# Attention scores in runs of one and a half key tiles over six PSUM banks

## The chip, the cores and the metric

The kernel runs on one core of one Trainium2 chip. The metric is the time of one execution on the device in microseconds (us), the median of several. TensorE (PE in the profile; PEld its weight loads), VectorE (DVE), ScalarE (ACT), GpSimd (POOL) and SyncE (SP, which issues most DMA transfers) each work through a queue of their own, in order, and wait for one another through semaphores. TensorE writes into PSUM, eight banks of 128 partitions by 512 float32 numbers, from which ScalarE and VectorE read.

## What is computed

Two layers, each of an attention block and a spectral filter, on 2048 rows of 1024 numbers:

```python
def _A_ref(x, wqkv, wo):                 # 32 heads of 32 numbers
    qkv = (x @ wqkv).reshape(B, S, 3, H, Dh) ...
    scores = einsum("bhqd,bhkd->bhqk", q, k) * (Dh ** -0.5)
    p = softmax(scores)
    o = einsum("bhqk,bhkd->bhqd", p, v)
    return o.transpose(...).reshape(B, S, D) @ wo
x = x + _A_ref(layernorm(x), wqkv, wo)
x = x + _B_ref(layernorm(x), w_r, w_i)   # rfft2, times a weight, irfft2
x = x + _A_ref(layernorm(x), wqkv, wo)
x = x + _B_ref(layernorm(x), w_r, w_i)
```

The change touches the attention block alone.

## The kernel before

**Tiles.** The 32 heads are worked on in eight groups of four (g = 0 to 7), the 2048 queries in four chunks of 512 (c), the 2048 keys in 16 tiles of 128 (kt). One *unit* is one (g, c, kt): 64 units a group. Float32 products are made of float16 parts, high and low, in three terms: high by high, high by low, low by high. The head's 32 numbers are the contraction, so the score matmuls use strips of 32 rows of the array, one strip for each head of the group.

**A unit.** `S` (line 697) makes the scores of a unit: three terms by four heads, each a matmul of 32 rows, 128 keys and 512 queries. They go into two tiles `s` of the pool `psS`, each of two banks and two heads; the pool has three such tiles, six banks in all. `S` also issues two exps on ScalarE (line 701), one for each tile, into tiles `p` of a pool of eight. `PV` (line 707) multiplies four heads' `p` by V, 128 rows by 32 columns, in float32, two passes each, into one bank `o`, accumulated over the 16 key tiles of the chunk. `add` (lines 718 and 720) sums `p` over the key tiles into `acc` on VectorE, two instructions of 128x1024 a unit. At a chunk's end `fin` (from line 727) sums `acc` over partitions with a matmul by ones, turns and inverts the sums on VectorE, and scales the output; `out` splits it into float16 parts (line 740 on ScalarE, 741 on VectorE) and stores it through SyncE's queue (line 743).

**What goes between.** Beside the units, TensorE makes q, k and v of later groups. `filler` yields step by step: a sum of q or k (`qk_chunk`, line 420) is 24 matmuls of 512 columns in 24 steps, a sum of v (`v_tiles`, line 465) 48 of 256 columns in 24 steps; both accumulate in the only tile `x` of the pool `psX`. At a sum's end the result is split: a high part by ScalarE (line 215), a low part by VectorE (line 216); for q and k the square of the high part is taken as well, for norms (line 427 on VectorE, line 425 on ScalarE where g is 7). Even groups make k, q and k (12 sums), odd groups 1, 3 and 5 make q and v (4 and 8 sums), group 6 makes k and q of group 7 and begins with the output projection (`wo_parts`, line 526). `prep` loads the weights of the next phase in pieces (line 301, SyncE) into three buffers and splits each (lines 215, 216). When the four sums of a phase are done, `norms` (line 440) adds the squares up by a matmul into a tile of `psS`, and VectorE takes the maximum (line 442), from which the exp's bias comes.

**Order.** TensorE's and ScalarE's instructions are issued in the order of the program; a planner orders the other queues by when it believes that things are ready. The order is: `S` of a unit; with every even unit the `PV` of the two units before it; with every odd unit a slot of filler, eight steps mostly and twelve at times (`slots` spreads the sums over the group). At the first unit of a chunk `fin` of the chunk before follows its last `PV`. In the trace, TensorE's order is therefore: S, PV PV, S, filler, S, PV PV, S, filler.

Of the kernel before, what the change touches and what calls it, by code (L numbers as in the profile page):

```python
# [104 lines left out]
SQ = 2.0 ** 5  # L105
# [131 lines left out]
class AttnPools:  # L237


    def __init__(self, tc):  # L240
        self.tc = tc
        self.low = Pools(tc, "left")
        self.big = self.low("at_x", 1).tile([128, 16384], F32, name="big")
        self.right = Pools(tc, "right")
        r = self.right("at_r", 1).tile([128, 16384], F32, name="R")
        self.x = r.rearrange("p (t d) -> p t d", d=1024)
        k = r.bitcast(F16).rearrange("p (t a n) -> p t a n", a=2, n=2048)
        self.k = [k[:, i] for i in (3, 4, 5)]
# [3 lines left out]
        a = r.rearrange("p (a j n) -> p a j n", j=2, n=512)  # L252
        self.acc = [a[:, i] for i in (14, 15)]

    def close(self):
        self.small.close()
# [19 lines left out]
class Weights:  # L276
# [6 lines left out]
    def prep(self, ph, mid=None):  # L283
        nc, ap, wp = self.nc, self.ap, self.wp
        kind, g = ph
        if kind == "v":
# [19 lines left out]
            load()  # L306
        yield
        for i, (h, l, _) in enumerate(sl):
            split(nc, h, l, st[i], SW)
            load()  # L310
            yield
        if self.flag is not None:
            v = w[:, 0].rearrange("p d n -> p (d n)")
# [17 lines left out]


SPILL = [2, 3, 8, 9]
PH0 = [("v", 0), ("k", 0), ("q", 0)]


def attention(nc, tc, layer, ap, xin, yd, wts, wo, cst, dram, flags):
# [69 lines left out]
    def qk_chunk(ph, c):  # L407
# [13 lines left out]
            if i < 23:  # L421
                yield
        split(nc, t[:, 0], t[:, 1], ps, SQ / (SX * SW))
        if g == NG - 1:
            nc.scalar.activation(nrm[ph][:, c], t[:, 0], AF.Square)
        else:
            (nc.gpsimd if both else nc.vector).tensor_tensor(nrm[ph][:, c], t[:, 0], t[:, 0], op=ALU.mult)
        if c == 3:
            left_norms.append(ph)
        yield  # L430

    left_norms = []

    def norms():
        kind, g = ph = left_norms.pop(0)
        if g not in mx:
            mx[g] = sm.tile([128, 2], F32, name="mqk")
        ps = psS.tile([128, 2, 512], F32, name="s")
        for c in range(4):
            nc.tensor.matmul(ps[32 * c:32 * c + 32, 0], cst["bones"], nrm[ph][:, c], start=True, stop=True)  # L440
        i = 0 if kind == "k" else 1
        nc.vector.reduce_max(mx[g][:, i:i + 1], ps[:, 0], axis=AX.X)  # L442
        if kind == "q":
            mkbias(g)

# [31 lines left out]
    def sums(ph):  # L477
        return 8 if ph[0] == "v" else 4

    def filler():  # L480
        for i, ph in enumerate(phases[:-2]):
            nxt = (s for p in phases[i + 1:i + 2 + (i + 4 > len(phases))] for s in prep(p))
            for n in range(sums(ph)):
# [202 lines left out]
    both.clear()  # L686


    P, O, acc = {}, {}, ap.acc

    def S(g, c, kt):

        s = [psS.tile([128, 2, 512], F32, name="s") for _ in range(2)]
        for i, (a, b) in enumerate(((0, 0), (0, 1), (1, 0))):
            for h in range(4):
                r = slice(32 * h, 32 * h + 32)
                nc.tensor.matmul(s[h // 2][:, h % 2], K[g][r, a, kt * 128:kt * 128 + 128],  # L697
                                 Q[g][r, b, c * 512:c * 512 + 512], start=i == 0, stop=i == 2)
        for hf in range(2):
            p = P[g, c, kt, hf] = pp.tile([128, 2, 512], F32, name="p")  # L700
            nc.scalar.activation(p, s[hf], AF.Exp, bias=bias[g], scale=SCALE / (SQ * SQ))  # L701

    def PV(g, c, kt):
        if kt == 0:
            O[g, c] = psO.tile([128, 512], F32, name="o")
        for h in range(4):
            nc.tensor.matmul(O[g, c][32 * h:32 * h + 32], V[g][:, kt, 32 * h:32 * h + 32], P[g, c, kt, h // 2][:, h % 2],  # L707
                             start=kt == 0, stop=kt == NKT - 1)
# [5 lines left out]
    def add(g, c, kt):  # L714
        for hf in range(2):
            p = P[g, c, kt, hf]
            if kt == 1:
                nc.vector.scalar_tensor_tensor(acc[hf], P[g, c, 0, hf], 1e-34, p, op0=ALU.add, op1=ALU.add)  # L718
            elif kt:
                last_add = nc.vector.tensor_add(acc[hf], acc[hf], p)  # L720
        return last_add if kt > 1 else None

    def fin(g, c):
        zt = on.tile([128, 16, 32], F32, name="zt")
        z = psS.tile([128, 2, 512], F32, name="s")[:, 0]
        for h in range(4):
            nc.tensor.matmul(z[32 * h:32 * h + 32], cst["ones"], acc[h // 2][:, h % 2], start=True, stop=True)  # L727
        nc.vector.transpose(zt.rearrange("p a b -> p (a b)"), z)  # L728
        rc = sm.tile([128, 16], F32, name="rc")
        nc.vector.reciprocal(rc, zt[:, :, 0])  # L730
# [3 lines left out]
        nc.vector.scalar_tensor_tensor(r, O[g, c], SO, r, op0=ALU.mult, op1=ALU.mult)  # L734
        O[g, c] = r

    def out(g, c, eng=nc.vector):
# [3 lines left out]
        eng.tensor_tensor(t[:, 1], r, t[:, 0], op=ALU.subtract)  # L741
        if g < NG - 1:
# [4 lines left out]
    pend, done, late = [], [], []  # L747
    fill, lwo, wof = filler(), load_wo(), wo_parts()
    left, rests = 16, {}
# [4 lines left out]
    def slots(f, sums, n, steps):  # L754

        while sums:
            k = max(1, int(n / sums + 0.5))
            m = -(-steps // k)
            for i in range(0, steps, m):
                while left_norms:  # L760
                    norms()
                for _ in range(min(m, steps - i)):
                    next(f, None)
                n -= 1
                yield sums - (i + m >= steps)
            sums -= 1

    with tc.manual_schedule(engines={mybir.EngineType.PE, mybir.EngineType.Activation}):
        for g in range(NG):
            todo = sum(sums(ph) for ph in beside.get(g, []))  # L770
            sl = slots(fill, todo, 22 if g == NG - 2 else 32, 24)
            wsl = slots(wof, 4, 10, 21)
            for u in range(NCH * NKT):
                c, kt = divmod(u, NKT)
                S(g, c, kt)
                if g == u == 0:
                    run(last_v)
                if kt % 2 == 0:
                    for w in pend:
                        PV(*w)  # L780
                    late = pend
                    pend = []
                    if kt == 0 and late:
                        for w in late:
                            last_add = add(*w)
                        with tc.issue_after(last_add.ins):
                            wts.look()
                        done = [late[1][:2]]
                        fin(*done[0])
                        late = []  # L790
                for w in late[:1]:
                    add(*w)
                late = late[1:]
                if kt == 5 and done:
                    out(*done.pop())
                pend.append((g, c, kt))
                if kt % 2 == 0:
                    continue
                if todo:
                    todo = next(sl)  # L800
                elif g == NG - 2:
                    if left:
                        run(lwo)
                        left = 0
                    if next(wsl, None) is not None and u == NCH * NKT - 1:
                        run(wsl)
                elif g == NG - 1:
                    for _ in range(share[u // 2]):
                        next(wof)
                    if u // 2 in rests:  # L810
                        wo_rest(rests[u // 2])
                if g == NG - 2 and todo <= 6 and left > (8 if todo > 4 else 0):
                    next(lwo)
                    left -= 1
        for w in pend:
            PV(*w)
        for w in late + pend:
# [3 lines left out]
    with tc.manual_schedule(engines={mybir.EngineType.PE}):  # L821
# [40 lines left out]
            for _ in range(n):  # L862
                next(folds, None)
        first(0, range(7))
        fin(NG - 1, NCH - 1)
        out(NG - 1, NCH - 1, nc.vector)
        some(6)
        first(1, range(7))
# [512 lines left out]
```

## Time and profile before

| | |
|---|---|
| median of 3 runs | 3764.36 us (3763.21 to 3766.41) |
| the profiled execution | 3764.43 us, its span 3762.6 us |
| TensorE busy | 3695.4 us, 98% of the span |
| VectorE busy | 3218.8 us, 86% |
| ScalarE busy | 2900.2 us, 77% |
| GpSimd busy | 298.8 us, 8% |
| granted TensorE clock, mean | 0.996 |
| 2048 exps (line 701) | 2170.0 us busy, 1112 ns each |
| 1792 additions (line 720) | 2088.6 us busy, 1220 ns each |
| head groups 1 to 6 of the first layer | 178.0 to 180.2 us each |

Busy times of one engine are added up over the span; durations of neighbouring instructions on an engine overlap a little, so what one costs is the distance from its start to the next start. TensorE's ends are modelled: a matmul of 512 columns is shown 0.38 us long, while the next starts 0.22 us after it. In a timeline row, the first number is the start, the second the length of the merged instructions, then engine, line, operation, output and inputs, and how many were merged; in brackets stands idle time of the engine and who ended it.

### The profile page before, as it was taken

Reading aid. Unit: us, or ns where it says so; the run is one execution under the profiler, and the core shown is the slowest. Engines: PE = TensorE matmul, PEld = TensorE weight load, DVE = VectorE, ACT = ScalarE, POOL = GpSimd, SP = SyncE. Lnnn points to the kernel's source line nnn. Section 1 sums busy time; section 2 is a strip of 40 time slices with the busy share of each in tenths; the row PEclk is TensorE's granted clock in tenths of the full one; section 3 lists DMA queues with packets and bytes.
Section 4 is the critical chain, followed back from the end, with each engine's and each line's share of the span. In section 5 each row is a group of like instructions: output and inputs, shape, how many; then the busy total and the mean of one; then the engine's idle time right before and its main releaser. Section 6 shows DMA issues by size and latency. Waiting matters only on the chain.

```text
span 3762.6 us, 80259 instructions
## 1 busy us (share of the span) xinstructions
PE 3695.4 (98%) x33271; PEld 1637.1 (44%) x33271; DVE 3218.8 (86%) x3874; ACT 2900.2 (77%) x3587; POOL 298.8 (8%) x388
## 2 busy tenths in 40 slices
PE   8999999999999999999999999999999999999998
PEld 5333433343343333378963334333433433333788
DVE  7899899989999988975658998999899999789755
ACT  5788888888888866658748888888888888666686
POOL 1000000000000000014410000000000000000243
PEclk9999999999999999999999999999999999999999
DMA  6000000000000211233250000101000102111423
GB/s 194 10 18 18 13 13 17 26 7 18 13 27 15 88 54 65 74 143 106 70 157 21 29 29 24 32 24 35 14 29 29 41 15 85 54 71 68 166 86 109
DMA packets 150119, 198.43 MB, mean 53 GB/s; under 512 B 58224, under 2 KB 104048, under 8 KB 148720
## 3 DMA queue, kind: packets, MB, share of 16 engines
q1 hardware_dynamic: 148416, 192.62, 15.8%
q8 instruction: 263, 4.31, 0.5%
q14 instruction: 112, 0.92, 0.1%
q10 hardware_dynamic: 1328, 0.59, 0.1%
HBM read 132.35 MB, written 48.23 MB: 48 GB/s over the span
## 4 chain that ended last, share of the span: by engine, by line


## 5 line engine op out<-in xcount | busy, mean ns | idle before, releaser
L701 ACT ACTIVATE p<-s,bias 128x1024 f32<-128x1024 f32 x2048 | 2170.0, 1112 | 563.0 <-PE s L697 545.6
L720 DVE TENSOR_TENSOR R<-R,p 128x1024 f32<-128x1024 f32 x1792 | 2088.6, 1220 | 131.2 <-ACT p L701 126.8
L707 PE MATMUL o<-p,R 128*32 128x512 f32 x8192 | 985.0, 598 | 0.0
L420 PE MATMUL x<-big,wqk 128*128 128x512 f16 x2880 | 676.5, 380 | 2.3 <-ACT R L469 1.9
L697 PEld LDWEIGHTS <-R 32*128 32x128 f16 x12288 | 230.9, 92 | 749.2 <-issue 633.5
L420 PEld LDWEIGHTS <-wqk 128*128 128x128 f16 x3072 | 275.6, 98 | 418.4 <-issue 129.3
L707 PEld LDWEIGHTS o<-p,R 128*32 128x32 f32 x8192 | 213.6, 109 | 523.4 <-issue 523.4
L697 PE MATMUL s<-Q,R 32*128 32x512 f16 x6144 | 427.3, 377 | 4.6 <-DVE R L567 2.7
L697 PE MATMUL s<-R 32*128 32x512 f16 x6144 | 430.4, 377 | 1.5 <-ACT p L701 0.3
L465 PE MATMUL x<-wv,big 128*128 128x256 f16 x2784 | 330.6, 275 | 4.1 <-DVE R L216 2.2
L465 PEld LDWEIGHTS <-big 128*128 128x128 f16 x3072 | 290.9, 98 | 100.2 <-issue 59.3
L526 PE MATMUL x<-big 128*128 128x512 f16 x1050 | 241.6, 380 | 0.0
L448 POOL PARTITION_ALL_REDUCE mall<-mqk x16 | 38.4, 2401 | 2278.1 <-DVE mqk L442 2266.7
L526 PEld LDWEIGHTS <-big 128*128 128x128 f16 x1344 | 124.3, 98 | 176.4 <-issue 38.6
L718 DVE SCALAR_TENSOR_TENSOR R<-p 128x1024 f32<-128x1024 f32 x128 | 150.8, 1218 | 31.8 <-ACT p L701 31.8
L1043 DVE TENSOR_TENSOR H<-G,H 128x512 f16<-128x512 f32 (+1 forms) x68 | 47.0, 692 | 119.8 <-ACT H L1042 119.6
L988 ACT COPY U<-ps 64x256 f32<-64x256 f32 (+1 forms) x272 | 97.2, 357 | 9.2 <-PE ps L995 3.9
L988 ACT COPY B<-ps 64x256 f32<-64x256 f32 (+1 forms) x272 | 97.2, 357 | 5.4 <-PE ps L995 1.7
L995 PE MATMUL ps<-cbi,H 128*128 128x256 f16 (+1 forms) x792 | 98.6, 273 | 1.5 <-DVE H L1043 1.0
L728 DVE STREAM_TRANSPOSE zt<-s 128x512 f32<-128x512 f32 x64 | 45.8, 715 | 62.6 <-PE s L727 62.5
L995 PE MATMUL ps<-cb,big 128*128 128x256 f16 x780 | 96.7, 273 | 0.0
L995 PEld LDWEIGHTS <-H 128*128 128x128 f16 (+1 forms) x792 | 76.5, 98 | 12.4 <-DVE H L1043 2.4
(443 smaller groups left out, 2981.7 us busy)
## 6 DMA issues: line engine op xcount, KB each, us to landing
wst<-in_wp SPq DMA_DIRECT2D x96, 256.0 KB, 3.0
R<-y SPq DMA_DIRECT2D x32, 512.0 KB, 5.2
w<-in_w SPq DMA_DIRECT2D x60, 256.0 KB, 2.7
od<-ohl SPq DMA_DIRECT2D x56, 256.0 KB, 2.4
big<-od SPq DMA_DIRECT2D x16, 896.0 KB, 5.9
y<-R SPq DMA_DIRECT2D x20, 512.0 KB, 2.6
wst<-in_wo SPq DMA_DIRECT2D x32, 256.0 KB, 2.7
xres<-in_x SPq DMA_DIRECT2D x16, 512.0 KB, 3.6
```

The costliest lines, as they stand in the source:

```text
L420: nc.tensor.matmul(ps, a, b, start=i == 0, stop=i == 23)
L465: nc.tensor.matmul(ps[:, j], x[c][:, d, o:o + 128], w[:, n, d], start=i == 0, stop=i == 23)
L526: nc.tensor.matmul(p, a, b, start=start and d == ds[0] and i == 0, stop=stop and d == ds[-1] and i == 2)
L697: nc.tensor.matmul(s[h // 2][:, h % 2], K[g][r, a, kt * 128:kt * 128 + 128], Q[g][r, b, c * 512:c * 512 + 512], start=i == 0, stop=i == 2)
L701: nc.scalar.activation(p, s[hf], AF.Exp, bias=bias[g], scale=SCALE / (SQ * SQ))
L707: nc.tensor.matmul(O[g, c][32 * h:32 * h + 32], V[g][:, kt, 32 * h:32 * h + 32], P[g, c, kt, h // 2][:, h % 2], start=kt == 0, stop=kt == ...
L718: nc.vector.scalar_tensor_tensor(acc[hf], P[g, c, 0, hf], 1e-34, p, op0=ALU.add, op1=ALU.add)
L720: last_add = nc.vector.tensor_add(acc[hf], acc[hf], p)
L728: nc.vector.transpose(zt.rearrange("p a b -> p (a b)"), z)
L988: nc.scalar.copy(ov[64 * r:64 * r + 64, a0:a0 + m, x], tl[64 * x:64 * x + 64, :m, r])
L995: nc.tensor.matmul(out, l, r, start=k == 0, stop=k == len(mm_) - 1)
L1043: nc.vector.tensor_sub(lo, gs, hi)
```

## The change

In groups 0 to 6, the 16 units of a chunk are made in ten runs `S3` and one plain `S`. An S3 makes the scores of one whole unit and of one half (256 queries) of another: of each three key tiles, the first and the third are whole units, the middle one is made in two halves. It takes all three tiles of `psS`: `y` (heads 2, 3 of the whole unit), `z` (four heads of the half unit, two heads in each bank) and `x` (heads 0, 1 of the whole unit), and three exps follow in the order y, z, x. The order of its 24 matmuls is written out in `RUN`: heads 0 and 1 begin with their half, heads 2 and 3 with their whole. The two pairs use the banks of `z` one after the other; a wait goes over SyncE's queue, a `nop` that waits for heads 0 and 1 and for which heads 2 and 3 wait.

Three `PV` units follow every second run, fillers of twelve steps follow the other runs and the first. The last unit of a chunk is left over and multiplied in the first run of the next, with `fin` behind it. Half units have `PV` of 256 columns and an addition `add_half` of both pairs of heads at once. The norms' matmuls move in between the `PV` units and write into the bank of the fillers; squares are made on ScalarE for all q and k within these groups. SyncE's queue joins the ones in program order, the output is stored two runs after its split, and `prep` loads a weight piece ahead of the next split instead of behind the last. Group 7 keeps the old order.

```diff
-        self.acc = [a[:, i] for i in (14, 15)]
+        self.acc = r.rearrange("p (a j n) -> p a j n", j=2, n=512)[:, 14:16]
...
         for i, (h, l, _) in enumerate(sl):
+            if late and i:
+                load()
             split(nc, h, l, st[i], SW)
-            load()
+            if not late:
+                load()
             yield
...
+TERMS = ((0, 0), (0, 1), (1, 0))
+RUN = [(h, i, z) for z, i, hs in ((1, 0, (0, 1)), (0, 0, (2, 3)), (1, 1, (0, 1)), (1, 2, (0, 1)), (0, 1, (2, 3)),
+                                  (0, 0, (0, 1)), (0, 2, (2, 3)), (0, 1, (0, 1)), (1, 0, (2, 3)), (1, 1, (2, 3)),
+                                  (0, 2, (0, 1)), (1, 2, (2, 3))) for h in hs]
...
-        if g == NG - 1:
+        if both:
+            nc.gpsimd.tensor_tensor(nrm[ph][:, c], t[:, 0], t[:, 0], op=ALU.mult)
+        else:
             nc.scalar.activation(nrm[ph][:, c], t[:, 0], AF.Square)
-        else:
-            (nc.gpsimd if both else nc.vector).tensor_tensor(nrm[ph][:, c], t[:, 0], t[:, 0], op=ALU.mult)
...
-    def norms():
+    def norms(z=None):
...
+        z = psS.tile([128, 2, 512], F32, name="s")[:, 0] if z is None else z
         for c in range(4):
-            nc.tensor.matmul(ps[32 * c:32 * c + 32, 0], cst["bones"], nrm[ph][:, c], start=True, stop=True)
+            nc.tensor.matmul(z[32 * c:32 * c + 32], cst["bones"], nrm[ph][:, c], start=True, stop=True)
...
+    def S3(g, c, kt, kz, qh):
+        y, z, x = (psS.tile([128, 2, 512], F32, name="s") for _ in range(3))
+        zv = z.rearrange("p j (s q) -> p j s q", q=256)
+        for h, i, half in RUN:
+            r, (a, b) = slice(32 * h, 32 * h + 32), TERMS[i]
+            o, k, q, n = ((zv[:, h % 2, h // 2], kz, c * 512 + 256 * qh, 256) if half else
+                          ((x, y)[h // 2][:, h % 2], kt, c * 512, 512))
+            m = nc.tensor.matmul(o, K[g][r, a, k * 128:k * 128 + 128], Q[g][r, b, q:q + n], start=i == 0, stop=i == 2).ins
+            if (h, i, half) == (1, 2, 1):
+                turn = nc.sync.nop(nofuse=True).ins
+                tc.add_manual_dep(turn, m.name, sync, reason="the first row tiles are done with the bank")
+            if (h, i, half) == (2, 0, 1):
+                tc.add_manual_dep(m, turn.name, sync, reason="the last row tiles follow in the same bank")
+        P[g, c, kt, 1] = exp(g, pp.tile([128, 2, 512], F32, name="p"), y)
+        p = exp(g, pp.tile([128, 2, 512], F32, name="p"), z)
+        Z[g, c, kz, qh] = p.rearrange("p j (s q) -> p s j q", q=256)
+        P[g, c, kt, 0] = exp(g, pp.tile([128, 2, 512], F32, name="p"), x)
...
+    def add_half(g, c, kt, q):
+        sl = slice(256 * q, 256 * q + 256)
+        if kt == 1:
+            for hf in (1, 0):
+                nc.vector.scalar_tensor_tensor(acc[:, hf, :, sl], P[g, c, 0, hf][:, :, sl], 1e-34, Z[g, c, kt, q][:, hf],
+                                               op0=ALU.add, op1=ALU.add)
+        else:
+            nc.vector.tensor_add(acc[:, :, :, sl], acc[:, :, :, sl], Z[g, c, kt, q])
...
+    def slot(g, n):
+        if g < NG - 2 or n < 16:
+            for _ in range(0 if g == n == 0 else 24 if g == 0 and n == 1 else 12):
+                next(fill)
+        else:
+            for _ in range(11 - n % 2):
+                next(wof)
+
+    def chunk(g, c):
+        for r in range(11):
+            i, b = divmod(r, 2)
+            n = 6 * c + (r + 1) // 2
+            if r < 10:
+                S3(g, c, 3 * i + 2 * b, 3 * i + 1, b)
+            else:
+                S(g, c, 15)
...
+            if r and not b:
+                for k in range(3):
+                    PV(g, c, 3 * i - 3 + k)
+                    if k == 1 and r in (2, 6, 10):
+                        while left_norms:
+                            norms(bank())
+            if r == 0 and pend:
+                PV(*pend[0])
+                boundary(pend.pop())
+            if r == 2 and done:
+                stores.append(out(*done.pop(), store=False))
+            if r == 4 and stores:
+                store(*stores.pop())
+            if r:
+                i, k = divmod(r - 1, 2)
+                if r > 2:
+                    add(g, c, 3 * i + 2 * k, (1,))
+                add_half(g, c, 3 * i + 1, k)
+                add(g, c, 3 * i + 2 * k, (0,) if r > 2 else (1, 0))
+            if b or r == 0:
+                slot(g, n)
+            if g == NG - 2 and 4 <= n + (b or r == 0) and left and (left.pop(0) % 3 < 2):
+                next(lwo)
+        pend.append((g, c, 15))
+
+    with tc.manual_schedule(engines={mybir.EngineType.PE, mybir.EngineType.Activation, mybir.EngineType.SP}):
+        for g in range(NG - 1):
+            for c in range(NCH):
+                chunk(g, c)
```

`boundary` adds the left-over unit up and calls `fin`; `PV` of a half unit makes eight matmuls of 256 columns where a whole one makes four of 512.

More of the change, by code (lines that the diff above doesn't have):

```diff
@@ L475, in attention @@
     phases = [ph for g in range(NG - 1) for ph in beside[g]]
-    def sums(ph):
-        return 8 if ph[0] == "v" else 4
     def filler():
         for i, ph in enumerate(phases[:-2]):
-            nxt = (s for p in phases[i + 1:i + 2 + (i + 4 > len(phases))] for s in prep(p))
-            for n in range(sums(ph)):
+            nxt = (s for p in phases[i + 1:i + 2 + (i + 4 > len(phases))] for s in prep(p, late=True))
+            for n in range(8 if ph[0] == "v" else 4):
                 yield from (v_tiles if ph[0] == "v" else qk_chunk)(ph, n)
@@ L699, in S @@
         for hf in range(2):
-            p = P[g, c, kt, hf] = pp.tile([128, 2, 512], F32, name="p")
-            nc.scalar.activation(p, s[hf], AF.Exp, bias=bias[g], scale=SCALE / (SQ * SQ))
+            P[g, c, kt, hf] = exp(g, pp.tile([128, 2, 512], F32, name="p"), s[hf])
     def PV(g, c, kt):
@@ L735, in fin, with store, out @@
         O[g, c] = r
-    def out(g, c, eng=nc.vector):
+    def store(g, c, t):
+        nc.sync.dma_start(od[:, g, :, c * 512:(c + 1) * 512].rearrange("a p n -> p a n"), t)
+    def out(g, c, eng=nc.vector, store=True):
         r = O.pop((g, c))
@@ L741, in out @@
         eng.tensor_tensor(t[:, 1], r, t[:, 0], op=ALU.subtract)
+        if not store:
+            return g, c, t
         if g < NG - 1:
@@ L745, in out @@
             olast[c] = t
-    pend, done, late = [], [], []
+    pend, done, stores = [], [], []
     fill, lwo, wof = filler(), load_wo(), wo_parts()
-    left, rests = 16, {}
+    left, rests = list(range(24)), {}
     share = [21] * 10 + [7] * 6 + [11, 10] * 6 + [12] * 4
@@ L752, in attention @@
         rests[n] = t
[L754 to L766, printed above, removed]
-    with tc.manual_schedule(engines={mybir.EngineType.PE, mybir.EngineType.Activation}):
[L769 to L814, printed above, removed]
@@ new lines, in slot, with boundary @@
+    def slot(g, n):
[5 more added lines that the diff above has]
+                next(wof)
+    def boundary(w):
+        last_add = add(*w)
+        with tc.issue_after(last_add.ins):
+            wts.look()
+        done.append(w[:2])
+        fin(*w[:2], psS.tile([128, 2, 512], F32, name="s")[:, 0])
+    def chunk(g, c):
[6 more added lines that the diff above has]
+                S(g, c, 15)
+            if g == c == r == 0:
+                run(last_v)
+            if r and not b:
[22 more added lines that the diff above has]
+        pend.append((g, c, 15))
@@ new lines, in attention @@
+    with tc.manual_schedule(engines={mybir.EngineType.PE, mybir.EngineType.Activation, mybir.EngineType.SP}):
+        for g in range(NG - 1):
+            for c in range(NCH):
+                chunk(g, c)
+    g = NG - 1
+    with tc.manual_schedule(engines={mybir.EngineType.PE, mybir.EngineType.Activation}):
+        for u in range(NCH * NKT):
+            c, kt = divmod(u, NKT)
+            S(g, c, kt)
+            if kt % 2 == 0:
+                for w in pend:
+                    PV(*w)
+                late, pend = pend, []
+                if kt == 0:
+                    for w in late[:-1]:
+                        add(*w)
+                    boundary(late[-1])
+                    late = []
+            for w in late[:1]:
+                add(*w)
+            late = late[1:]
+            if kt == 5:
+                out(*done.pop())
+            pend.append((g, c, kt))
+            if kt % 2:
+                for _ in range(share[u // 2]):
+                    next(wof)
+                if u // 2 in rests:
+                    wo_rest(rests[u // 2])
@@ L864, in attention @@
         first(0, range(7))
-        fin(NG - 1, NCH - 1)
+        fin(NG - 1, NCH - 1, psS.tile([128, 2, 512], F32, name="s")[:, 0])
         out(NG - 1, NCH - 1, nc.vector)
```

37 lines of the change are left out of this document (21 added, 16 removed).

## The prediction

> **What bounds the kernel now.** I read the page first (shares, granted clock), then busy time by stretch, one stretch for each of three head groups of the first layer, then the order of time on TensorE and on the engines that feed it.
>
> ```profile
> span 3762.6 us, 80259 instructions
> ...
> PEclk9999999999999999999999999999999999999999
> ...
> 462.50:640.50 178.00, 178.00 (x1612) 54.55 (x1613) 168.40 (x179) 148.34 (x154) 2.29 (x4) 1.00 0.05 16
> 640.50:820.70 180.20, 179.40 (x1804) 73.57 (x1807) 164.22 (x167) 148.67 (x162) 7.07 (x4) 1.00 0.05 16
> 1178.90:1357.60 178.70, 177.78 (x1600) 54.23 (x1596) 169.53 (x176) 155.07 (x169) 2.29 (x4) 1.00 0.17 56
> ```
>
> The columns are length, then busy time of PE, PEld, DVE, ACT and POOL. The rows are group 2 (an even group), group 3 (odd) and group 6. TensorE is never idle; VectorE has 9 to 16 us a group to spare, ScalarE 24 to 32. So a group's length is the sum of TensorE's work, the clock being full. What this work is made of:
>
> ```profile
> 491.12 0.82 PE L697 MATMUL s<-R 32*128 32x512 f16 x12
> 491.88 1.90 PE L420 MATMUL x<-big,wqk 128*128 128x512 f16 x8
> 493.71 0.83 PE L697 MATMUL s<-R 32*128 32x512 f16 x12
> 494.46 1.93 PE L707 MATMUL o<-p,R 128*32 128x512 f32 x16
> 496.32 0.83 PE L697 MATMUL s<-R 32*128 32x512 f16 x12
> ...
> 529.33 0.40 PE L440 MATMUL s<-sq,bones 128*32 128x512 bf16 x4
> 529.66 1.90 PE L420 MATMUL x<-big,wqk 128*128 128x512 f16 x8
> ...
> 545.57 2.76 PE L420 MATMUL x<-big,wqk 128*128 128x512 f16 x12
> 548.27 0.83 PE L697 MATMUL s<-R 32*128 32x512 f16 x12
> 549.02 1.92 PE L707 MATMUL o<-p,R 128*32 128x512 f32 x16
> 550.77 1.04 PE L727 MATMUL s<-R,ones 128*32 128x512 f32 x8
> 551.74 0.83 PE L697 MATMUL s<-R 32*128 32x512 f16 x12
> ...
> 725.65 2.79 PE L465 MATMUL x<-wv,big 128*128 128x256 f16 x24
> 728.38 0.83 PE L697 MATMUL s<-Q,R 32*128 32x512 f16 x12
> ```
>
> Read starts, not lengths: a score unit S (12 matmuls, one key tile) occupies 0.76 us until what follows, eight filler steps 1.83, twelve 2.70, two PV units 1.86, two PV units and the sums of `fin` (a third set of the same form) 2.72, the norms' matmuls 0.33. Twelve less eight steps give 0.2175 us a step, so 1.83 holds 0.09 us that is no stream: the price of going from one array shape (128*128) to another (32*128). In the same way S pays 0.76 less three streams of 0.2175, 0.11, and a PV pair 1.86 less twice 0.86 (2.72 less 1.86), 0.14. A 256-column step costs (2.73-0.09)/24 = 0.11. Every change of shape costs about 0.1 us and TensorE makes 32 in each chunk of 512 queries, which is what this change works on.
>
> **The change part by part.** Runs of a chunk are numbered r = 0 to 10: ten S3 (one unit and half of another) and one S. Fillers of twelve steps follow at r = 0, 1, 3, 5, 7, 9, three PV units at r = 2, 4, 6, 8, 10, the last PV unit of the chunk before and `fin` at r = 0.
>
> (1) Fewer changes of shape. S3 has on each strip of 32 rows three matmuls of 512 columns and three of 256: 0.76+3x0.11 = 1.09. Chunk after: r=0 1.09+1.86+2.70 = 5.65; five odd runs 1.09+2.70 = 3.79; four even runs 1.09+2.72 = 3.81; r=10 0.76+2.72 = 3.48; sum 43.3. Chunk before: 16x0.76 + 7x1.86 + 2.72 + 72x0.2175 + 8x0.09 = 44.3. The norms move among column-shaped PV work and pay 0.22 for 0.33, 0.08 a chunk. That is 1.08 a chunk, 4.3 a group. Halved PV matmuls of five units a chunk stream as many columns, twice as many instructions; no row has them. Bounds: nothing, and 0.09 a unit (as if each unit paid a change of shape), 25 us in all; I take nothing, as 256-column steps pay 0.001 over half a 512.
>
> (2) Waits of before that go. Group 3 is 2.2 longer than group 2; its 256-column fillers explain 16x0.03 = 0.5, so 1.7 are waits. Group 6 has twelve filler steps fewer (2.6) and yet is 0.7 longer: 3.3 of waits. New waits are priced below, so these go first. Gain per layer: groups 0, 2, 4 4.3 each, groups 1, 3, 5 6.0 each, group 6 7.6: 38.5, in two layers 77 us. Group 7 and all else stays.
>
> (3) The score banks. S used four of six and left two to go on with; S3 uses six, so a run waits for the exps of the last one.
>
> ```profile
> 491.98 2.12 ACT L701 ACTIVATE p<-s,bias 128x1024 f32<-128x1024 f32 x2 [0.49 <-PE s L697]
> ...
> 678.03 1.15 ACT L215 ACTIVATE wv<-wst 128x512 f16<-128x512 f32 x2
> 679.07 2.12 ACT L701 ACTIVATE p<-s,bias 128x1024 f32<-128x1024 f32 x2
> ...
> 1195.31 0.61 ACT L215 ACTIVATE R<-x 128x512 f16<-128x512 f32 x1
> 1195.95 0.63 ACT L425 ACTIVATE sq<-R 128x512 bf16<-128x512 f16 x1
> 1196.48 3.11 ACT L701 ACTIVATE p<-s,bias 128x1024 f32<-128x1024 f32 x3
> ```
> ```profile
> 1197.07 0.39 PE L697 MATMUL s<-R 32*128 32x512 f16 x2
> 1197.63 0.82 PE L697 MATMUL s<-R 32*128 32x512 f16 x10 [0.17 <-ACT p L701]
> ```
>
> The exp of a finished half starts 0.86 after its S (491.12 to 491.98), two take 2.12, three 3.11, and TensorE takes a bank up again 0.05 after its exp (1196.48+1.10 to 1197.63). In S3 the second pair of heads has its 512 columns done where an S has, so exps run from 0.86 to 3.97 after the run's start and the last tile is free at 4.02. The next run (3.80 later) needs it only after its 256-column third, at 4.13: 0.1 to spare. ScalarE is free at 3.89 and the next exp is ready at 3.80+0.86 = 4.66: 0.77 for other work costs nothing.
>
> A filler sum of q or k ends with a split (0.61) and, new, the square: from 1195.31 to 1196.48 = 1.17, so the next exps are 0.40 late and the run after waits 0.40-0.10 = 0.30. At r=9 the one plain S absorbs it. Eight such waits in groups 0, 2, 4, three in 1, 3, 5: 66 in two layers, 20 us. A weight split of two halves (678.03 to 679.07 = 1.04) costs 0.17, 18 times: 3 us; at r=0, a long run, it is free. Group 6 adds the output weights' splits (0.52 each, two runs of three from late in the first chunk): of its six sums that count, two wait 0.30 and four 0.65 on average (0.82 with such a split), 3.2 a layer, 6 us. The V copies and `oc`, `ohl` stay under 0.77. The eight buffers of `p` are not the limit: in an even run the third exp takes the buffer that its first PV unit frees at 1.09+0.86 = 1.95, and starts at 2.9. Ends: nothing, and every other ScalarE operation at its full length beside a run already tight, 1.17 for each of the 66, 77 us.
>
> (4) VectorE loses 0.33 to 0.42 a square and has 10 us a group over; two halves instead of one at the first addition cost it 0.1 a pair. At the chunk's change `fin` needs the last unit's additions:
>
> ```profile
> 545.97 3.49 DVE L720 TENSOR_TENSOR R<-R,p 128x1024 f32<-128x1024 f32 x3
> ...
> 551.88 0.72 DVE L728 STREAM_TRANSPOSE zt<-s 128x512 f32<-128x512 f32 x1 [1.29 <-PE s L727]
> ```
>
> Today VectorE is 1.29 early there. An addition comes every 1.14. After: the S of r=10 has its exps done 3.4 after its start (0.86+0.40+2.12), additions 4.6; TensorE asks at 3.48+1.09+0.86 = 5.4. I take 0.1 a chunk, 6 us (0 to 1.0, 56). The norms now write the fillers' single bank, which VectorE empties behind additions: 0.3 for each of 28, 8 us (0 to 1).
>
> (5) SyncE's queue, now in program order. Each S3 has a wait there between the two uses of a shared bank. The first use ends 0.54 after the run's start (third 256 at 0.24, plus 0.86-0.45-0.11), the second starts at 0.66, so 0.12 are left for SyncE to pass it on.
>
> ```profile
> 679.72 1.29 DVE L216 SCALAR_TENSOR_TENSOR wv<-wst,wv 128x512 f16<-128x512 f32 x2
> ...
> 680.43 0.93 SPq L301 DMA_DIRECT2D wst<-in_wp  x2
> ```
>
> SyncE issues a load 0.03 after VectorE's 0.68 ends, TensorE hears in 0.05: 0.08 in all, hidden. Ends: 0, and 0.3 a run (a wait as long as an issue, 0.93 for two with a gap), 168 us for 560 runs. I take 0, being nearest the 0.03 row. What would stand behind a late one: the run's last four steps on TensorE, its PV or filler, and two exps. The output store goes out two runs after its split, the output weights' loads a run after the split that frees their buffer: data ready, and an issue is over before the next run's wait. The fourth V weight load is the exception: it waits in SyncE until the first half is split, and the next run's wait stands behind it. ScalarE reaches that half at 3.89, done 4.5; VectorE, after the run's last addition, at 5.2 to 5.8; the issue ends at 6.2, where the run asked for it at 3.80+0.66: 1.7 us, three per layer: 10 us (1.0 to 4.8 each).
>
> **Sum.** -77 +20+3+6 +6+8 +10 = -24 against the profiled 3764.43 us (span 3762.6), 0.07 over the median 3764.36: 3740.
>
> [...]
>
> **The rivals.** (a) The other side: SyncE's hop is late. From 0.12 on every run is longer; a hop of 0.22 costs 560x0.10 = 56, less 7 in the waits of (3): 3789. For it: 0.04 of margin, no row of such a hop. Against: 0.03 and 0.05 of its two ends. Chance 0.15. (b) VectorE is the bound at the chunk's change: 1 us in each of 56 instead of 0.1 gives 3790. For it: 3.4 us of additions in each 3.8 us run. Against: 10 us spare. 0.10. (c) The waits of (3) do not come, ScalarE finding room: 3740-29 = 3711, less the V loads 3701. 0.13. (d) Strips of unequal matmuls don't overlap: each of a run's steps takes the longest, 1.28 instead of 0.96, 560x0.32 = 179: 3919. Nothing shows unequal strips; 12 matmuls of S take 0.83 together, each strip on its own. 0.04. (e) The rule above, 3755: 0.03.
>
> **How the numbers follow.** The forecast has 0.55, own range 3720 to 3758. (c) and (a), (b) bound the range: 3702 to 3790, which leaves out (d) and the tails, under 0.2. Two runs of this kernel can be told apart from about 0.2%, 7.5 us. Faster: 0.49 of the forecast and (c), 0.62. Slower: (a), (b), (d), most of them, 0.25. Same: 0.13.
>
> **What would show it.** S3 at 1.09 to what follows, 23 changes of shape a chunk; groups 0, 2, 4 within 1 us of 178, 1, 3, 5 near 177.5, 6 near 175. Waits of TensorE on exps of 0.3 at r=3 and r=7, none at r=0. A wait on SyncE of over 1 us once in groups 1, 3, 5. If S3 takes 1.2 everywhere, (a); 1.4, (d); a gap ahead of `fin`, (b). A group under 175 says that the banks cost nothing and the forecast is too high.

## The result, and the profile after

| | before | after |
|---|---|---|
| median | 3763.78 us (4 runs) | 3869.18 us (4 runs) |
| ratio of after to before | | 1.0283, 95% interval 1.0265 to 1.0300 |
| profiled span | 3762.6 us | 3871.7 us |

The change makes the kernel 105 us slower; 3740 was forecast. From the page after, busy time, share of the span and instructions:

```profile
span 3871.7 us, 90485 instructions
...
PE 3695.9 (95%) x38871; PEld 1923.6 (50%) x38871; DVE 3237.9 (84%) x3890; ACT 2926.3 (76%) x3683; POOL 289.0 (7%) x388
```

VectorE at 84% does not look like the bound; in the first stretch below it has 170.52 of 186.30, 92%. Busy time by stretch for the same three groups (2, 3 and 6 of the first layer); the columns are length, then PE, PEld, DVE, ACT and POOL:

```profile
476.00:662.30 186.30, 178.41 (x2022) 75.14 (x2012) 170.52 (x178) 152.52 (x167) 4.06 (x4) 1.00 0.05 16
662.30:844.70 182.40, 176.94 (x2200) 93.80 (x2196) 163.74 (x167) 149.23 (x166) 4.07 (x4) 0.99 0.05 16
1214.70:1408.60 193.90, 179.31 (x1998) 73.98 (x1992) 171.95 (x185) 153.80 (x168) 1.75 (x4) 0.98 0.17 56
```

The groups are 8.3, 2.2 and 15.2 us longer. TensorE was never idle in group 2; now it is for 8 us of it. In order of time on TensorE, a quiet stretch of group 2:

```profile
482.18 2.76 PE L427 MATMUL x<-big,wqk 128*128 128x512 f16 x12
484.87 1.15 PE L709 MATMUL s<-R 32*128 32x256 f16 x24
485.96 2.79 PE L740 MATMUL o<-p,R 128*32 128x512 f32 x32
488.68 1.44 PE L709 MATMUL s<-R 32*128 32x256 f16 x24
490.05 0.39 PE L427 MATMUL x<-big,wqk 128*128 128x512 f16 x1
```

Twelve filler steps take 2.69, an S3 1.09, three PV units 2.72, within a hundredth what was forecast: unequal strips do overlap, the hop over SyncE is hidden, halved PV matmuls cost nothing. The S3 at 488.68, the fourth run of its chunk, takes 1.37: the forecast wait on an exp, 0.28 instead of 0.30. The plan of the change holds, and with it (1). What fails is elsewhere in the same group:

```profile
654.64 0.83 PE L726 MATMUL s<-R 32*128 32x512 f16 x12
655.40 1.93 PE L740 MATMUL o<-p,R 128*32 128x512 f32 x24
660.16 0.40 PE L447 MATMUL x<-sq,bones 128*32 128x512 bf16 x4 [2.83 <-DVE R L216]
660.38 1.04 PE L740 MATMUL o<-p,R 128*32 128x512 f32 x8
```

The norms' matmuls stand between the second and the third PV unit and wait 3.0 us (two PV units take 1.75: 660.16 less 655.40+1.75) for the bank that VectorE's half of the split (line 216) has to empty. VectorE at that time, additions of whole halves in line 752, of half units in line 763:

```profile
650.68 2.36 DVE L752 TENSOR_TENSOR R<-R,p 128x1024 f32<-128x1024 f32 x2
653.15 1.23 DVE L763 TENSOR_TENSOR R<-R,p 128x1024 f32<-128x1024 f32 x1
654.48 2.36 DVE L752 TENSOR_TENSOR R<-R,p 128x1024 f32<-128x1024 f32 x2
656.95 1.23 DVE L763 TENSOR_TENSOR R<-R,p 128x1024 f32<-128x1024 f32 x1
658.28 1.23 DVE L752 TENSOR_TENSOR R<-R,p 128x1024 f32<-128x1024 f32 x1
659.42 0.68 DVE L216 SCALAR_TENSOR_TENSOR R<-x,R 128x512 f16<-128x512 f32 x1
```

It is not idle, it is behind, and one run of additions takes it 656.95-653.15 = 3.80 us, as long as TensorE's run of 3.79. Two of three additions come 1.33 after the one before (653.15 to 654.48), the third 1.14 (2.36-1.22 in a merged pair). The slow ones are those that read what was written just before: the half unit's addition reads and writes the sums of both pairs of heads, so it depends on the addition of `y` ahead of it, and that of `x` behind depends on it. The trace shows how they wait, in semaphore instructions that a timeline leaves out: the addition of 653.15 ends at 654.38, at 654.42 stands a wait of VectorE on its own semaphore, and the next addition starts at 654.48. In the kernel before, the additions took the pairs in turn:

```profile
470.05 4.62 DVE L720 TENSOR_TENSOR R<-R,p 128x1024 f32<-128x1024 f32 x4
```

Four in 4.62, (4.62-1.22)/3 = 1.13 apart. The chain's 0.19 us is paid twice a run from the fourth run on (the first two half units go through line 760 instead), 16 times a chunk, 3.0 us. That is 12 us a group, where group 2 had 9.6 to spare. The idle column does not name it, since each instruction is as long as before (1220 and 1226 ns on average, 1220 before the change).

The same lateness shows in SyncE's queue. This is the fourth load of a V weight in group 3, with TensorE, VectorE and the queue:

```profile
694.26 0.93 PE L709 MATMUL s<-Q,R 32*128 32x256 f16 x16
699.35 0.50 PE L709 MATMUL s<-Q,R 32*128 32x256 f16 x8 [4.16 <-SPq L711]
699.78 4.48 PE L740 MATMUL o<-p,R 128*32 128x512 f32 x32
704.19 1.15 PE L709 MATMUL s<-Q,R 32*128 32x256 f16 x22
```
```profile
698.20 1.29 DVE L216 SCALAR_TENSOR_TENSOR wv<-wst,wv 128x512 f16<-128x512 f32 x2
...
698.91 0.33 SPq L300 DMA_DIRECT2D wst<-in_wp  x1
```

The S3 stops after sixteen matmuls, where the wait over SyncE stands; the load ahead of it in that queue starts when VectorE's split ends, 698.20+0.68, and frees the queue at 699.24.

The PV behind it takes 4.41 us (699.78 to 704.19) instead of 2.72, without waiting. The row of busy time from 700.0 to 703.4 shows why, in the third number from the end, the granted clock:

```profile
700.00:703.40 3.40, 3.40 (x28) 1.27 (x24) 2.50 (x3) 2.12 (x2) 0.00 (x0) 0.50 0.21 76
```

TensorE is at half its clock. In the trace after, such stretches, mostly of 3.4 or 6.8 us, make 79 us, in that of before 27 (the mean granted clock is 0.990 and 0.996). Each of those in the attention blocks begins within 2.3 us of the end of a wait of TensorE of 2.2 us or more, though not every such wait has one (the 3.0 us at the norms above has none). At half the clock, the 52 us more are up to 26 of the 105 us, an estimate that no run tests alone. They are a second price of the long waits, and the table below counts them at the places where they fall.

Over the trace I took each stretch of TensorE from its start to the next start and subtracted its quiet length (S3 1.09, filler 2.70, and so on). Both layers:

| place | waits, us | forecast |
|---|---|---|
| norms at r = 6 and 10, until the bank is free | 31 | 8 with the next row |
| fillers behind norms, until the maximum is taken (lines 427 and 472 in the list of waits) | 22 | |
| ahead of `fin` | 10 | 6 |
| ninth run of groups 1, 3, 5: V load, and PV behind it | 38 | 10 |
| group 6, first matmuls of the projection | 16 | 0 |
| exps at r = 3 and 7 (66 of 0.28) | 18 | 20 |

The rest, some 40, is spread over `fin`'s neighbours and group 6. All in all 178 against 53 forecast. 178 less 77 is 101, near the 105 measured, so the 77 us of (1) and (2) hold as a sum; the share of (2), the waits of before that go, has no row of its own.

### The profile page after: what moved, and what is told of

The parts are those of the page before. It is cut to its first block, busy times and chain, and to the rows that moved or that the text cites. A ratio compares the mean times of both kernels' runs of the same rounds, so it can differ in the third digit from the quotient of the medians.

```text
span 3871.7 us, 90485 instructions
## 1 busy us (share of the span) xinstructions
PE 3695.9 (95%) x38871; PEld 1923.6 (50%) x38871; DVE 3237.9 (84%) x3890; ACT 2926.3 (76%) x3683; POOL 289.0 (7%) x388
## 4 chain that ended last, share of the span: by engine, by line
## 5 line engine op out<-in xcount | busy, mean ns | idle before, releaser
L696 ACT ACTIVATE p<-s,bias 128x1024 f32<-128x1024 f32 x2048 | 2138.8, 1111 | 657.0 <-PE s L709 427.9
L752 DVE TENSOR_TENSOR R<-R,p 128x1024 f32<-128x1024 f32 x1344 | 1595.5, 1220 | 105.0 <-ACT p L696 59.3
L740 PE MATMUL o<-p,R 128*32 128x512 f32 (+1 forms) x10432 | 980.5, 510 | 0.0
L709 PEld LDWEIGHTS <-R 32*128 32x128 f16 x13440 | 380.3, 92 | 503.7 <-issue 361.3
L763 DVE TENSOR_TENSOR R<-R,p 128x1024 f32<-128x1024 f32 x448 | 549.0, 1226 | 50.5 <-ACT p L696 3.5
L740 PEld LDWEIGHTS o<-p,R 128*32 128x32 f32 x10432 | 300.8, 110 | 420.2 <-issue 327.2
L709 PE MATMUL s<-R 32*128 32x512 f16 (+1 forms) x7680 | 389.1, 323 | 12.2 <-SPq L711 7.9
L709 PE MATMUL s<-Q,R 32*128 32x512 f16 (+1 forms) x5760 | 285.6, 325 | 25.2 <-SPq L711 25.0
L760 DVE SCALAR_TENSOR_TENSOR R<-p 128x512 f32<-128x512 f32 x224 | 145.3, 669 | 119.2 <-ACT p L696 119.2
L726 PE MATMUL s<-Q,R 32*128 32x512 f16 x1824 | 125.6, 377 | 2.7 <-DVE R L571 2.7
L726 PEld LDWEIGHTS <-R 32*128 32x128 f16 x2208 | 41.1, 92 | 124.9 <-issue 104.1
L768 PE MATMUL s<-R,ones 128*32 128x512 f32 x512 | 87.7, 609 | 14.3 <-DVE R L752 9.7
```

The source lines that it names most:

```text
L696: nc.scalar.activation(p, s, AF.Exp, bias=bias[g], scale=SCALE / (SQ * SQ))
L709: m = nc.tensor.matmul(o, K[g][r, a, k * 128:k * 128 + 128], Q[g][r, b, q:q + n], start=i == 0, stop=i == 2).ins
L740: nc.tensor.matmul(O[g, c][r, q], V[g][:, kt, r], src, start=kt == 0, stop=kt == NKT - 1)
L752: last_add = nc.vector.tensor_add(acc[:, hf], acc[:, hf], p)
L760: nc.vector.scalar_tensor_tensor(acc[:, hf, :, sl], P[g, c, 0, hf][:, :, sl], 1e-34, Z[g, c, kt, q][:, hf], op0=ALU.add, op1=ALU.add)
L763: nc.vector.tensor_add(acc[:, :, :, sl], acc[:, :, :, sl], Z[g, c, kt, q])
```

## The experiments

**Theory 1**: the chain of additions makes VectorE the bound, and the waits stand wherever TensorE needs VectorE. **Theory 2**: the places are at fault (the fillers' bank for norms, SyncE's order) at any pace of VectorE. **Theory 3**: ScalarE, with the squares, is short beside exps that all six banks wait for.

### No chain: e1_no_chain

```diff
-            nc.vector.tensor_add(acc[:, :, :, sl], acc[:, :, :, sl], Z[g, c, kt, q])
+            for hf in range(2):
+                nc.vector.tensor_add(acc[:, hf, :, sl], acc[:, hf, :, sl], Z[g, c, kt, q][:, hf])
```

> The changed kernel, but a half unit's addition is two instructions of 512 instead of one of 1024, each on one pair of heads, in the order pair 0, pair 1, so that no addition reads what the one just before it wrote. Theory 1 (each addition that reads the sum just written waits 0.19 us for it, twice a run, so VectorE needs 3.80 us for a run of 3.79, falls behind, and all that waits for it is late: norms, fin, the fourth V load): additions 1.14 apart again, the waits at the norms, at fin and behind the V load shrink to about what was forecast, 3740 to 3775 us. Theory 2 (the waits come from where the change put things: norms into the fillers' bank, loads into SyncE's program order, whatever VectorE's pace): within 20 us of the changed kernel, 3850 to 3875.

3786.4 us, ratio to before 1.0062 (1.0045 to 1.0079): 83 us of the 105 are gone. That is 11 less than theory 1's range asked, and far outside theory 2's. VectorE, in order of time:

```profile
628.84 1.28 DVE L764 TENSOR_TENSOR R<-R,p 128x512 f32<-128x512 f32 x2
630.04 2.35 DVE L752 TENSOR_TENSOR R<-R,p 128x1024 f32<-128x1024 f32 x2
632.31 1.28 DVE L764 TENSOR_TENSOR R<-R,p 128x512 f32<-128x512 f32 x2
```

A run of additions takes 632.31-628.84 = 3.47 instead of 3.80, though it has an instruction more. Groups 2, 3 and 6:

```profile
465.50:644.40 178.90, 176.40 (x2017) 74.67 (x2012) 166.44 (x207) 152.58 (x166) 7.05 (x4) 1.00 0.05 16
644.40:822.90 178.50, 175.09 (x2206) 93.30 (x2196) 162.81 (x201) 149.17 (x166) 11.22 (x4) 1.00 0.05 16
1182.00:1368.50 186.50, 177.54 (x1998) 73.61 (x1992) 169.62 (x216) 153.59 (x168) 7.73 (x4) 0.98 0.18 59
```

Group 2 now stands 1 us from its forecast; groups 3 and 6 keep waits that are there without the chain, below.

### A chain in the kernel before: b1_chain_before

```diff
+                prev = last_add if hf else None
                 last_add = nc.vector.tensor_add(acc[hf], acc[hf], p)
+                if prev is not None:
+                    tc.add_manual_dep(last_add.ins, prev.ins.name, sync, reason="as if it read what the first wrote")
```

> The kernel before, with one wait more in each unit: the second addition waits for the first, as if it read its result; the sums are the same. Theory 1: 15 gaps of 0.19 us a chunk take VectorE from some 42.5 to 45.4 us, over TensorE's 44.5, so head groups get 3 to 6 us longer and the time is 3810 to 3860 us. Theory 2: VectorE has 9 us a group to spare and the old order bears it: under 10 us more, 3764 to 3774.

3825.95 us, ratio 1.0164 (1.0147 to 1.0181), 62 us more, as theory 1 said. Additions in order of time:

```profile
479.77 7.43 DVE L723 TENSOR_TENSOR R<-R,p 128x1024 f32<-128x1024 f32 x6
```

Six in 7.43, (7.43-1.22)/5 = 1.24 apart: one by one, two of the five distances are 1.14, two 1.32 and one 1.27. The second addition reads nothing that the first wrote, so the 0.19 us is the price of waiting for the end of the instruction just before. There are 14 such waits a chunk, not the 15 expected, 2.7 us. So the old order too has no room for 3 us a chunk, though 10 us a group looked idle on VectorE.

### Squares on GpSimd: e2_pool_squares

```diff
-        if both:
-            nc.gpsimd.tensor_tensor(nrm[ph][:, c], t[:, 0], t[:, 0], op=ALU.mult)
-        else:
-            nc.scalar.activation(nrm[ph][:, c], t[:, 0], AF.Square)
+        nc.gpsimd.tensor_tensor(nrm[ph][:, c], t[:, 0], t[:, 0], op=ALU.mult)
```

> The changed kernel with the squares for the norms on GpSimd instead of ScalarE. Theory 1: TensorE's 0.3 us waits on exps at the fourth and eighth run go, but VectorE remains the bound and takes most of it back: 3845 to 3865 us. Theory 3 (ScalarE, loaded with the squares beside exps that all six banks wait for, is what is short): 3869 less about 60, 3800 to 3815.

3943.91 us, ratio 1.0476 (1.0458 to 1.0493): 75 us slower than the change, which no theory expected. VectorE's additions (grouped, mean ns of one):

```profile
L749 DVE TENSOR_TENSOR R<-R,p 128x1024 f32<-128x1024 f32 x1344 | 1632.1, 1247 | 107.9 <-ACT p L693 62.2
L760 DVE TENSOR_TENSOR R<-R,p 128x1024 f32<-128x1024 f32 x448 | 567.8, 1267 | 51.5 <-ACT p L693 5.3 <-DVE R L749 0.5
```

1247 and 1267 ns, where the changed kernel has 1220 and 1226: GpSimd, multiplying, slows VectorE, by 27x1344+41x448 ns = 55 us here. All of it lies in the 213 additions that overlap a square: they take 1.44 us (line 749) and 1.62 us (line 760) on average, the others 1.22 and 1.23. TensorE's low clock grows too, from 79 to 159 us at 0.50, up to 40 us more by an estimate. So ScalarE's relief is mixed here with two new prices, and this run alone does not decide on theory 3. What speaks against it as the main cause is e1, where ScalarE keeps the squares and 83 us go. The additions beside a square are the only ones that got longer; by what mechanism, no run shows.

### V loads that wait for no split: e3_four_stages and c1_stages

The same edit, in the change and in the kernel without the chain:

```diff
-        self.sgp = small("at_stage", 3)
+        self.sgp = small("at_stage", 4)
...
-        for n in range(4 if self.flag is not None and ph in PH0 else 3):
+        for n in range(4):
```

> The changed kernel with four staging buffers for weights and all four pieces of a V load issued at once, so that no load waits in SyncE for a split. Theory 1: the 6.3 us at the ninth run of groups 1, 3 and 5 go, and part of it returns at the next place that needs VectorE: 15 to 35 us less, 3834 to 3854. Theory 2: all of the six waits of 6.3 us are gained, 38 us, 3831 or a little less.

> The kernel without chained additions, with four staging buffers so that no V load waits in SyncE for a split. Theory 1 (VectorE was the bound, and without the chain what is left are waits at a few places): the whole 21.7 us that the ninth runs of groups 1, 3, 5 still lose in six places go, 3762 to 3768. Rival (VectorE is still behind, and takes it back elsewhere): 10 us or less, 3776 and more.

In the change: 3850.45 us (ratio 1.0225, 1.0208 to 1.0242), 19 of the 38 us, so half of it comes back elsewhere, as theory 1 said. Without the chain: 3765.2 us (1.0005, 0.9996 to 1.0014), 21 of 21.7, all of it. Here a wait on VectorE's result was worth its length only where VectorE was not the bound.

### The output's load earlier: c2_output_load

On top of c1:

```diff
-        load_o(0)
         load_o(1)
...
+            if g == NG - 2 and c == 2 and r == 0:
+                load_o(0)
             if b or r == 0:
                 slot(g, n)
```

> The same, and the first load of the attention's output for the projection is issued at the first run of the third chunk of group 6 instead of at the eighth, four runs ahead of the matmuls that read it. If SyncE's program order is what makes TensorE wait there: 15 us less, 3747 to 3755. If the load waits for the data of the last stores anyway: no change, 3762 to 3768.

3751.19 us, ratio 0.9968 (0.9957 to 0.9979): 14 us less, and 0.3% under the kernel before. Not all of it is the wait itself, 4.5 us in c1 at the longest: behind it, c1 has 6.8 us a layer at a granted clock of 0.50 (from 1299 and from 3169), and c2 has none there. Groups 2, 3 and 6:

```profile
461.80:640.70 178.90, 176.39 (x2018) 74.65 (x2012) 166.46 (x207) 152.58 (x166) 6.87 (x4) 1.00 0.05 16
640.70:816.80 176.10, 174.93 (x2206) 93.41 (x2196) 162.59 (x201) 149.19 (x167) 10.38 (x4) 1.00 0.05 17
1171.80:1351.90 180.10, 175.56 (x1997) 73.40 (x1992) 169.42 (x216) 153.57 (x168) 12.57 (x4) 1.00 0.18 61
```

### The chain alone: d2_chain_alone

c2 with the half unit's addition as one instruction again.

> The version with four stages and the early output load, but with the half unit's addition as one instruction of 1024 again, as in the change. Theory 1: the chain by itself puts VectorE behind, whatever else is mended: 60 to 85 us over 3751, 3811 to 3836, with the waits at the norms and at fin back. Theory 2, of which the V load and the output load were two places: what is left of its cost is under 25 us, 3776 at most.

3837.52 us, ratio 1.0194 (1.0180 to 1.0208): 86 us over c2, a little over theory 1's range; theory 2 falls for most of the cost, beside the two places of c1 and c2. From the list of waits, engine and line, who is waited for, us in total, times and the longest:

```profile
PE s L767 <- DVE R L751: 24.8, 17, 2.6
...
PE x L447 <- DVE R L216: 16.9, 6, 2.8
PE x L447 <- DVE Q L216: 11.8, 8, 2.0
```

In c2 the last two are 3.4 and 1.4 us: `fin` and the norms' matmuls wait because VectorE is late, not because of the bank. One more place stays for theory 2, though. In c2, without the chain, the fillers behind the norms still wait for the maximum, 20 us where the changed kernel has 22:

```profile
PE x L427 <- DVE mqk L449: 12.7, 14, 1.1
...
PE x L472 <- DVE mqk L449: 6.9, 6, 1.1
```

### What is left of the waits: c3_dve_squares, c4_norms_score_bank, d1_late_squares

Each is c2 with one edit. c3 has the squares on VectorE, c4 the norms in the score banks, d1 has three of four squares behind the next run's exps:

```diff
c3
-            nc.scalar.activation(nrm[ph][:, c], t[:, 0], AF.Square)
+            nc.vector.tensor_tensor(nrm[ph][:, c], t[:, 0], t[:, 0], op=ALU.mult)
c4
-                            norms(bank())
+                            norms()
d1
-            nc.scalar.activation(nrm[ph][:, c], t[:, 0], AF.Square)
+            square = lambda o=nrm[ph][:, c], k=t[:, 0]: nc.scalar.activation(o, k, AF.Square)
+            squares.append(square) if c < 3 else square()
...
+            while squares:
+                squares.pop(0)()
```

> The same as with the output load early, and the squares back on VectorE. If ScalarE's squares cost 0.3 us at two of three sums, as forecast, and VectorE can bear 1 us more a chunk: 15 to 20 us less, 3730 to 3740. If VectorE is so near its limit that it falls behind again: longer by 10 us or more, 3758 and up.

> The same as with the output load early, and the norms' matmuls write a tile of the score banks, as in the kernel before, instead of the fillers' bank, which VectorE has to empty first. If the waits at the norms and behind them come from that bank: 10 us less, 3737 to 3745. If a seventh taker for six full banks costs the next run as much: within 5 us, 3745 to 3757.

> The version with four stages and the early output load, 3751 us, and of each four sums of a phase the first three have their square issued after the exps of the next run instead of at once; ScalarE then has one split of 0.5 us ahead of the next exps, not 1.17. If TensorE's 0.29 us waits at the fourth and eighth run come from the squares ahead of the exps: 56 of them go, 16 us, 3732 to 3738. If they come from the exps and the six banks alone: no change, 3748 to 3754.

c3: 3781.59 us (1.0048, 1.0034 to 1.0062), 30 more than c2. VectorE is still that near its limit: 0.33 us a square (from its start to the next start, line 427 in the kernel before), 1 us a chunk, is too much, and putting the squares on ScalarE is a right part of the change. By the same count of TensorE's stretches as above, the waits at r = 3 and 7 go, 19 us, while those at the norms and at `fin` grow from 11 to 49.

c4: 3785.56 us (1.0067, 1.0053 to 1.0080), 34 more, outside both ranges; the list of waits says why:

```profile
PE s L708 <- DVE mqk L449: 37.8, 28, 1.8
```

With all six banks taken, the next S3 cannot begin until VectorE has read the norms out, 28 times. The fillers' bank, which I doubted, is the better of the two places.

d1: 3749.78 us (0.9961, 0.9947 to 0.9974 on before), 1.4 less than c2, where 16 were forecast. By the same count of TensorE's stretches, the waits at r = 3 and 7 fall by 11 us in groups 0, 2 and 4, and 8 of it come back at the norms, at `fin` and at other runs. Over all groups 18 us go and 16 come back. So the squares did cause these waits, as the first branch said, but the time is that of the second. At r = 4, where 0.18 us a time come back, it is ScalarE once more: the late square and the output's cast (line 785) stand in a row ahead of the exps of r = 3. Why `fin` and the norms wait longer was not traced.

## Why the prediction was wrong

By its own steps:

- (1), the array's changes of shape: right to 0.01 us for S3, filler and PV. With (2), which was not measured by itself, the 77 us fit the sum of the waits, and are outweighed.
- (3), score banks and squares: right, 0.28 us a wait for 0.30, at r = 3 and 7 and not at r = 0 or behind r = 9. In c2, taking these waits away gained only 1.4 us (d1).
- **(4), VectorE: the step that failed.** It counted instructions and lengths ("an addition comes every 1.14") and priced the half unit at two halves of the first addition. It did not look at what each addition has to wait for, and so put the chain at nothing. The new addition writes both pairs' sums and stands between one that writes the first and one that writes the second, so two of three additions wait 0.19 us. That is 3.0 us a chunk, some 170 us of VectorE in 56 chunks, against 9 us a group of slack, 126 in all; the runs put 83 (e1) and 86 us (d2) of kernel time on it.
- The waits of the norms' matmuls (31 us in the changed kernel, 31 in d2, 8 in c2) and at `fin` follow from that. The fillers behind the norms do not: their 22 us are 20 in c2 too, so the 8 us that the prediction gave to the norms in the fillers' bank were some 20 too few at any pace of VectorE. Rival (b) named the engine and the sign and gave 3790; but it had no mechanism, looked for the wait at the chunk's change, where the table has 10 of the 178 us, took 10 us of idle time for room, and at 1 us a chunk was too small.
- (5), SyncE: the hop is hidden, as taken. The V load is the queue wait that was named, 6.3 us with the PV behind it (4.6 of wait and 1.7 of low clock) where 1.7 was forecast, because VectorE was late; in the kernel without the chain it still cost 3.5 (21 us in six places), inside the bounds of 1.0 to 4.8. The projection's first load was not named at all: in the order by hand it is issued when TensorE needs it, and costs 14 us.
- The granted clock was taken as full throughout. Behind the long waits it was 0.50, a price that no term had.
- (e), 3755, a price of its own for matmuls that increment a semaphore: no run shows one; S3 takes the 1.09 us that was summed without it.

The chain, the V load and the late load are 83, 21 and 14 of the 129 us between forecast and result. Without them, c2 gains 12 us of the 24 forecast. In the first layer, groups 2 and 3 are then 178.9 and 176.1, near or under their forecast, and group 6 is 180.1 where 175 was said. What is left against the forecast was not traced further; c3 and b1 say that VectorE stays close behind TensorE.

## What to carry to other kernels

Before a sum is merged or its slices are cut another way, write down for each instruction of that engine whether it has to wait for the one just before: work that alternates between two accumulators hides a wait that a single, overlapping accumulator pays each time (here 1.14 us from start to start against 1.33). VectorE, shown 95% busy by lengths in group 2, had no room here: ask for the distance from start to start, and test the room by adding a wait to the old kernel. A long wait of TensorE can cost more than its length: look at the granted clock just behind it (here 0.50 for 3.4 us behind the 4.2 us of the V load). When a queue is put into program order, every load in it that waits for another engine stands ahead of the next handshake, so each needs a buffer that is long free (a fourth one gained 21 us in c1).

## What the runs showed of the hardware

An addition of 128x1024 on VectorE that waits for the end of the one before starts 1.33 us after it, any other 1.14, with the same shown length of 1.22 us. In b1 nothing is read of the one before, so the 0.19 us is the wait's; whether the hardware could do without the wait where the sum is read was not tried. In e1, starts are 0.60 us apart at 512 numbers ((630.04-628.84)/2) and 1.135 at 1024 ((632.31-630.04)/2), so 2x0.60-1.135, some 0.07 us an instruction, does not grow with the length, an estimate from these two lengths. What makes up the 0.07 was not shown; the 0.19 of a wait comes on top of it.

A multiplication of 128x512 on GpSimd beside the additions takes 1.49 us (`R`) or 1.68 (`Q`) instead of 1.04 (median, line 427 in the kernel before), and lengthens each addition that it overlaps by 0.22 to 0.39 us. Row strips of the array with matmuls of 256 and of 512 columns run side by side without loss: 24 of them take 1.09 us to the next instruction, as their columns and one change of shape give (0.76+3x0.11, from the rows of the kernel before). A wait passed from TensorE over SyncE back to TensorE takes 0.09 us, from the end of the matmul (which is modelled) to the start of the weight load that waits, the median of the runs S3 after the change. In the trace after, TensorE was granted half its clock (0.50) fifteen times for 3.4 or 6.8 us, each time from within 2.3 us of the end of a wait of 2.2 to 4.9 us.
